# Row sums of the gated rows taken earlier, one conversion moved to ScalarE, and an opening in half tiles

## The chip, the cores and the metric

One core of one Trainium2 chip. The metric is the time of one execution in device microseconds; smaller is better. Each timed execution also reports its span and its mean granted TensorE clock: 1.000 is full clock, 0.5 is half.

## The reference, cut to what matters

A block of a transformer over 2048 rows of 1024: layer norm, local attention, output product with a residual, layer norm, then a bilinear feed-forward with 3584 hidden columns.

```python
x = A_x
h = x + _A_ref(_layernorm(x, axis=-1), A_wqkv, A_wo)
h2 = h + _B_ref(_layernorm(h, axis=-1), B_w_gate, B_w_up, B_w_down)
# _B_ref: g = x @ w_gate; u = x @ w_up; return (g * u) @ w_down
```

The change touches the start (the first layer norm and the first product with `wqkv`) and the last down product.

## The kernel before: the parts concerned

The opening takes the first 512 rows as four row tiles. Each is normalized on VectorE, transposed on TensorE in two halves, copied out of PSUM (one half by ScalarE, one by VectorE) and multiplied with the first weight tile. That weight tile comes in two transfers of 512 KB: products 1 to 16 of a row tile need the first, 17 to 32 the second.

```python
load_x0(0)
load_x0(1)
load_w0(0, 4)          # first half of the weight tile
load_x0(2)
load_w0(4, 4)          # second half
load_x0(3)
# ... (13 products on a zero tile follow, to warm the array) ...
for t in range(4):
    if t < 3:
        first_half(t + 1, 0)
    first_norm(t)
    if t < 3:
        first_half(t + 1, 1)
    if t > 0:
        first_mm(t - 1, range(0, 6))
    first_transpose(t)
    first_copy(t)
    if t > 0:
        first_mm(t - 1, range(6, 8))
    if t < 3:
        first_rstd(t + 1)
```

The last down product works on two chunks of rows at once with seven products of half-size blocks in place of eight, in 16-bit floats. Weights and gated rows are scaled by powers of two that come from sums of absolute values. Row sums need one reduction on VectorE (`rows`), one product with ones on TensorE (`total`) and five small VectorE operations. The b and t tiles are quarters of the down weights and their differences; each is held as two tiles, such as t2a and t2b. dx and dy are the accumulators of this product in PSUM; h is the residual to which its results are added.

```python
conv_down(down["b12"])                                   # VectorE, 2 instructions
# ...
add_homes(t1v, Fv("b12"), Fv("b11"), ALU.subtract)       # VectorE, 2 of 1.94 us
scale_h.rows()                                           # VectorE, 2 small ones
conv_down(down["b21"])                                   # VectorE, 2
for q in range(4):
    dprod(ps_x[q], q, HA["11"], fcells(down["b11"]), True)   # TensorE, 14 products
    if q == 1:
        scale_h.total(ps_y[3])
        # ...
for q in range(4):
    nc.scalar.activation(ps_y[q][:], ps_x[q][:], ACTF.Copy, scale=sh)
# ... HF22, HF21 on VectorE, HF11 on ScalarE, S1 = HF21 + HF22 on VectorE ...
for q in range(4):
    dprod(ps_x[q], q, HA["12"], fcells(down["b21"]), False)
    result(2, q, 0, ps_x[q], scale_d.inv, None)          # VectorE, waits for dprod q
    if q == 2:
        conv_down(down["b22"])                           # VectorE, 2
# ... HF21 = HF11 - HF21, HF11 = S1 - HF11 on VectorE ...
add_homes(t2v, Fv("b22"), t1v, ALU.subtract)             # t2a, t2b
for q in range(4):
    dprod(ps_x[q], q, S1, cells(t1h), True)
# ...
for q in range(4):
    dprod(ps_y[q], q, HF["11"], cells(t2h), False)       # waits for t2a, then t2b
```

Of the kernel before, what the change touches and what calls it, by code (L numbers as in the profile page):

```python
# [8 lines left out]
BF = mybir.dt.bfloat16  # L9
# [3 lines left out]
ALU = mybir.AluOpType  # L13
# [5 lines left out]
D = 1024  # L19
# [59 lines left out]
def kernel(  # L79
# [11 lines left out]
    nc = tc.nc  # L91
# [9 lines left out]
    lnp = ctx.enter_context(tc.tile_pool(name="ln", bufs=4))  # L101
# [80 lines left out]
    def normalize(src, mv4, rs4, t):  # L182
        ln = lnp.tile([128, D], BF, tag="ln")
        nc.vector.tensor_scalar(ln[:], src[:], mv4[:, t, 0:1], rs4[:, t:t + 1], ALU.subtract, ALU.mult)
        return ln

    def ln_tiles(name):
        mv4 = small.tile([128, 4, nc.vector.BN_AGGR_DIM], F32, tag="mv4", name="mv" + name)
        rs4 = small.tile([128, 4], F32, tag="rs4", name="rs" + name)
        return mv4, rs4  # L190
# [9 lines left out]
    lnTs = {}  # L200
# [59 lines left out]
    x0 = [hp.tile([128, D], BF, tag="h", name=f"x0_{t}") for t in range(4)]  # L260
# [29 lines left out]
        nc.gpsimd.memset(mask[:, w, 0:DIL * w], NEG)  # L290

    wps = psum.tile([128, 512], F32, tag="mm", name="warm_ps")
    for i in range(13):
        nc.tensor.matmul(wps[:], lhsT=warm[:, 0:128], rhs=warm[:], start=True, stop=True)

    qkv_in = {}
# [19 lines left out]
    lnTs[0] = lnTp.tile([128, KO, TC], BF, tag="lnT", name="lnT1_0")  # L316
    mv0, rs0 = ln_tiles("1_0")

    pts = {}

    sts = {}

    def first_half(t, i):
        if i == 0:
            sts[t] = small.tile([128, 2, nc.vector.BN_STATS_DIM], F32, tag="st", name=f"st0_{t}")
        nc.vector.bn_stats(out=sts[t][:, i, :], in_=x0[t][:, bass.ts(i, 512)])

    def first_rstd(t):
        nc.vector.bn_aggr(out=mv0[:, t, :], in_=sts[t][:])
        rstd_of(mv0, rs0, t, t + 1)  # L330

    lns = {}

    def first_norm(t):
        lns[t] = normalize(x0[t], mv0, rs0, t)

    def first_transpose(t):
        for hf in range(2):
            pt = psum.tile([128, KO // 2, 128], BF, tag="mm", name=f"pt{t}_{hf}")
            for kk in range(KO // 2):  # L340
                nc.tensor.transpose(pt[:, kk, :], lns[t][:, bass.ts(4 * hf + kk, 128)], ident[:])
            pts[t, hf] = pt
        nc.scalar.copy(lnTs[0][:, 0:4, bass.ts(t, 128)], pts[t, 0][:])

    def first_copy(t):
        nc.vector.tensor_copy(lnTs[0][:, 4:8, bass.ts(t, 128)], pts[t, 1][:])

    def first_mm(t, kos):
        for ko in kos:
            for j in range(4):  # L350
                nc.tensor.matmul(ps0[j][:, bass.ts(t, 128)], lhsT=wts["qkv", 0][:, ko, bass.ts(j, 128)],
                                 rhs=lnTs[0][:, ko, bass.ts(t, 128)], start=(ko == 0), stop=(ko == KO - 1))
# [5 lines left out]
# [6 lines that stand above are left out]
        if t > 0:  # L364
            first_mm(t - 1, range(0, 6))
        first_transpose(t)
        first_copy(t)
        if t > 0:
            first_mm(t - 1, range(6, 8))
        if t < 3:  # L370
            first_rstd(t + 1)
# [187 lines left out]
    scale_gu, scale_d, scale_h = Scale("gu", 56), Scale("d", 56), Scale("h", 56)  # L559
# [216 lines left out]
    NH = NF // 4  # L776
# [8 lines left out]
    def to_f16(dst, src, sc, eng=nc.vector):  # L785
        if eng is nc.scalar:
            nc.scalar.activation(dst, src, ACTF.Copy, scale=sc)
        else:
            eng.tensor_scalar(dst, src, sc, None, ALU.mult)

    def f16(ap):
        return ap.bitcast(F16)

    def conv_down(homes):
        for t in homes:
            to_f16(f16(t[:, 0:NH, :]), t[:, 0:NH, :], scale_d.s)

    def cells(homes):
        return [t[:, k, :] for t in homes for k in range(NH)]
# [1 line left out]
    down = {}  # L801
    for n in range(NP):
        if n + 1 < NP:
            weight_sums(n + 1)
            if n + 2 < NP:
                load_pair(n + 2)
            else:
                names = ("b11a", "b12a", "b21a", "b21b", "b12b")
                ws = {k: home(wpool, "w", "dn_" + k, BF) for k in names}
                down["b11"] = [ws["b11a"], home(att, "oD", "dn_b11b", BF)]  # L810
                down["b12"] = [ws["b12a"], ws["b12b"]]
                down["b21"] = [ws["b21a"], ws["b21b"]]
                load_down(down["b11"], 0, 0)
                load_down(down["b12"], 0, 1)
        else:
            load_down(down["b21"], 1, 0)
        sums = [] if n == 0 else [
            (lambda n=n, k=k: abs_sum_h(n - 1, k, h23[4 * (n - 1) + k])) for k in range(4)]
        pair_block(n, h23[4 * n:4 * n + 4], sums)
        if n == NP - 2:  # L820
            conv_down(down["b11"])
# [9 lines left out]
    def add_homes(dst, x0, x1, op):  # L831
        for d, a0, a1 in zip(dst, x0, x1):
            nc.vector.tensor_tensor(d, a0, a1, op)
# [4 lines left out]
    def dprod(ps, q, lhs, rhs, fresh, lo=0, n=TC):  # L838
        for k in range(NP):
            nc.tensor.matmul(ps[:, bass.ds(lo, n)], lhsT=lhs[k][:, bass.ts(q, 128)], rhs=rhs[k][:, bass.ds(lo, n)],  # L840
                             start=(fresh and k == 0), stop=(k == NP - 1), skip_group_check=not fresh)

    def fcells(homes):
        return [f16(c) if c.dtype != F16 else c for c in cells(homes)]

    def result(c, q, hf, ps, sc, other, lo=0, n=TC):
        rows = (hs2 if c == 2 else hs3)[q]
        cols = bass.ds(hf * 512 + lo, n)
        nc.vector.scalar_tensor_tensor(rows[:, cols], ps[:, bass.ds(lo, n)], sc,
                                       rows[:, cols] if other is None else other[:, bass.ds(lo, n)], ALU.mult, ALU.add)  # L850
        nc.sync.dma_start(outf[bass.ds(c * TC + q * 128, 128), cols], rows[:, cols])


    conv_down(down["b12"])
    t1v = [t[:, 0:NH, :] for t in t1h]
    t2v = [t[:, 0:NH, :] for t in t2h]
    add_homes(t1v, Fv("b12"), Fv("b11"), ALU.subtract)
    scale_h.rows()
    conv_down(down["b21"])
    for q in range(4):  # L860
        dprod(ps_x[q], q, HA["11"], fcells(down["b11"]), True)
# [9 lines left out]
    for k in range(NP):  # L871
        to_f16(HF["22"][k], HA["22"][k], sh)
        to_f16(HF["21"][k], HA["21"][k], sh)
    s1h = [t[:, 0:NH, :] for t in down["b11"]]
    S1 = fcells(down["b11"])
    for k in range(NP):
        to_f16(HF["11"][k], HA["11"][k], sh, nc.scalar)
    for k in range(NP):
        nc.vector.tensor_tensor(S1[k], HF["21"][k], HF["22"][k], ALU.add)
    for q in range(4):  # L880
        dprod(ps_x[q], q, HA["12"], fcells(down["b21"]), False)
        result(2, q, 0, ps_x[q], scale_d.inv, None)
        if q == 2:
            conv_down(down["b22"])
    for k in range(NP):
        nc.vector.tensor_tensor(HF["21"][k], HF["11"][k], HF["21"][k], ALU.subtract)
    for k in range(NP):
# [60 lines left out]
```

## Time and profile before

| | before |
|---|---|
| time, median of 3 | 787.76 us |
| span of the profiled execution | 785.4 us |
| TensorE busy | 773.4 us, 98% |
| TensorE's waits that the profile names | 5.7 us in all |
| first full-width product (end of the opening) | 16.95 us |
| tail: first dx product to last dy product | 692.61 to 781.74, 89.13 us |

The prediction shows the lines and how they were read.

### The profile page before, as it was taken

What the parts mean: (1) busy time and instruction counts of PE and PEld (TensorE: products, weight loads), DVE (VectorE), ACT (ScalarE), POOL (GpSimd) and SP (SyncE); (2) the same over time, 40 slices, a digit from 0 to 9 for tenths busy, and PEclk for the clock granted to TensorE, in tenths of its full rate; (3) what the DMA queues carried; (4) which work ended last, traced back from release to release, by engine and by line L of the source; (5) the groups of instructions that cost most, each with busy time, mean ns of one, the idle gap of its engine ahead of it and who ended that gap; (6) DMA issues with size and microseconds to landing.
All of it is one profiled execution on the core that took longest, in us unless ns stands there. A gap on an engine that the chain in (4) does not pass through costs nothing.

```text
span 785.4 us, 10283 instructions
## 1 busy us (share of the span) xinstructions
PE 773.4 (98%) x3672; PEld 358.1 (46%) x3734; DVE 586.5 (75%) x729; ACT 394.8 (50%) x913; POOL 150.8 (19%) x160
## 2 busy tenths in 40 slices
PE   9999999999999999999999999999999999989998
PEld 6544444444444444444444444444444444434444
DVE  6629999999899998999979962724444453589862
ACT  4627445313676653956666510116777677645240
POOL 0000000100000200002000010067768668500000
PEclk9999999999999999999999999999999999999999
DMA  7999693996956868869455599533332332820001
GB/s 265 263 227 215 164 283 85 277 279 160 338 175 199 273 237 224 259 197 306 148 161 194 164 207 305 126 105 86 86 108 56 107 98 63 281 95 28 1 28 53
DMA packets 183683, 135.94 MB, mean 173 GB/s; under 512 B 79056, under 2 KB 176464, under 8 KB 181584
## 3 DMA queue, kind: packets, MB, share of 16 engines
q1 hardware_dynamic: 180048, 113.27, 51.0%
q0 software_dynamic: 3584, 22.02, 8.2%
q8 instruction: 29, 0.48, 0.3%
q14 instruction: 22, 0.18, 0.1%
HBM read 106.95 MB, written 22.02 MB: 164 GB/s over the span
## 4 chain that ended last, share of the span: by engine, by line
PE 75%; DVE 21%; issue 1%; SPq 1%; DMA 1%; ACT 0%; DVEq 0%
PE pu L389 12%; PE acc L608 12%; PE pg L389 12%; PE pz L661 6%; PE py L661 6%; PE px L661 6%; PE wo L510 5%; DVE prod L429 4%; PE ps L389 3%; PE dx L840 3%; PE pv L661 3%; PE dy L840 3%; DVE pv L472 2%; DVE prod L431 2%; SPq L223 1%
## 5 line engine op out<-in xcount | busy, mean ns | idle before, releaser
L389 PE MATMUL ps<-lnT,w_qkv 128*128 128x512 bf16 x721 | 158.9, 379 | 0.8
L389 PEld LDWEIGHTS <-w_qkv 128*128 128x128 bf16 x736 | 71.9, 98 | 85.9 <-issue 0.2
L389 PE MATMUL pu<-lnT,w_wu 128*128 128x512 bf16 x438 | 105.1, 379 | 0.6
L389 PE MATMUL pg<-lnT,w_wg 128*128 128x512 bf16 x440 | 105.1, 379 | 0.4
L608 PE MATMUL acc<-w_wd,gs 128*128 128x512 bf16 x438 | 96.7, 379 | 0.5
L300 ACT CAST sg<-ps 128x512 bf16<-128x512 f32 x96 | 54.8, 590 | 53.2 <-PE ps L389 49.4
L472 DVE TENSOR_TENSOR pv<-vD,at 128x4096 bf16<-128x4096 bf16 x32 | 72.5, 2287 | 0.3
L429 DVE TENSOR_TENSOR prod<-qD,kD 128x4096 bf16<-128x4096 bf16 x32 | 72.4, 2284 | 0.1
L608 PEld LDWEIGHTS <-gs 128*128 128x128 bf16 x448 | 43.8, 98 | 52.9
L661 PEld LDWEIGHTS <-sw 128*128 128x128 f16 x448 | 43.8, 98 | 52.8
L389 PEld LDWEIGHTS <-w_wg 128*128 128x128 bf16 x448 | 43.8, 98 | 52.9
L389 PEld LDWEIGHTS <-w_wu 128*128 128x128 bf16 x448 | 43.8, 98 | 52.9
L179 ACT ACTIVATE rs<-mv,eps 128x1 f32<-128x1 f32 x32 | 9.5, 296 | 102.0 <-DVE mv L176 98.2
L588 ACT CAST us<-pu 128x512 bf16<-128x512 f32 x56 | 33.1, 591 | 50.5 <-PE pu L389 49.3
L510 PE MATMUL wo<-w_wo,oT 128*128 128x512 bf16 x251 | 55.6, 379 | 0.3
L661 PE MATMUL px<-lnT,ws 128*128 128x512 bf16 x211 | 52.6, 379 | 0.6
L661 PEld LDWEIGHTS <-ws 128*128 128x128 f16 x336 | 32.9, 98 | 39.6
L484 POOL DMA_DIRECT2D od<-oD x4 | 2.2, 542 | 249.8 <-DVE oD L482 162.5
L640 POOL TENSOR_TENSOR sw<-ws 128x512 f16<-128x512 f16 x28 | 32.3, 1153 | 87.9 <-PE acc L608 47.2
L583 ACT CAST gs<-pg 128x512 bf16<-128x512 f32 x56 | 33.1, 591 | 12.8 <-PE pg L389 8.7
L510 PEld LDWEIGHTS <-oT 128*128 128x128 bf16 x256 | 25.0, 98 | 30.2
L431 DVE TENSOR_TENSOR prod<-prod 128x4096 bf16<-128x4096 bf16 x16 | 36.6, 2288 | 0.3
(244 smaller groups left out, 1189.4 us busy)
## 6 DMA issues: line engine op xcount, KB each, us to landing
w_wg<-in_B_w_gate_dram SPq DMA_DIRECT2D x14, 1024.0 KB, 6.9
w_wu<-in_B_w_up_dram SPq DMA_DIRECT2D x14, 1024.0 KB, 5.3
w_wd<-in_B_w_down_dram SPq DMA_DIRECT2D x16, 896.0 KB, 7.8
w_wo<-in_A_wo_dram SPq DMA_DIRECT2D x8, 1024.0 KB, 7.5
w_pair<-in_B_w_gate_dram SPq DMA_DIRECT2D x14, 512.0 KB, 4.0
w_pair<-in_B_w_up_dram SPq DMA_DIRECT2D x14, 512.0 KB, 5.3
w_qkv<-in_A_wqkv_dram SPq DMA_DIRECT2D x5, 1024.0 KB, 9.5
kd<-sg SPq DMA_DIRECT2D x32, 144.0 KB, 2.8
```

The costliest lines, as they stand in the source:

```text
L300: nc.scalar.copy(sg[:, HB:HB + TC], ps[:])
L389: nc.tensor.matmul(ps[:], lhsT=wt[:, ko, bass.ts(j, 128)], rhs=rhs[:, ko, :], start=(ko == 0), stop=(ko == KO - 1))
L429: nc.vector.tensor_tensor(prod[:, j], qD[:], kD[:, :, o:o + SUB], ALU.mult)
L431: nc.vector.tensor_tensor(prod[:, :, 0:16], prod[:, :, 0:16], prod[:, :, 16:32], ALU.add)
L472: nc.vector.tensor_tensor(pv[:, j], vD[:, :, o:o + SUB], at[:, w, None, :].to_broadcast((128, DH, SUB)), ALU.mult)
L510: nc.tensor.matmul(ps[:], lhsT=oTs[c][:, kk, t, :], rhs=wts["wo", c, hf][:, kk, :], start=(kk == 0), stop=(kk == KO - 1))
L583: nc.scalar.copy(gs[:], pg[:])
L588: nc.scalar.copy(us[:], pu[:])
L608: nc.tensor.matmul(acc[t][:], lhsT=hT[f][:, bass.ts(t, 128)], rhs=wts["wd", c, hf, b][:, j, :], start=(f == 0), stop=(f == NF - 1))
L640: nc.gpsimd.tensor_tensor(sw[:, i, 0], a21, a22, ALU.add)
L661: nc.tensor.matmul(ps[:], lhsT=lhs[:, ko, :], rhs=rhs[:, ko, :], start=(fresh and ko == 0), stop=(ko == 3), skip_group_check=not fresh)
L840: nc.tensor.matmul(ps[:, bass.ds(lo, n)], lhsT=lhs[k][:, bass.ts(q, 128)], rhs=rhs[k][:, bass.ds(lo, n)], start=(fresh and k == 0), stop=( ...
```

## The change

Its intent in the tail: take the row sums early enough that TensorE need not stop for them, and take the b22 conversion off VectorE. In the opening: shorter steps from a row tile to its first product, with two warm-up products fewer.

```diff
-    for i in range(13):
+    for i in range(11):
         nc.tensor.matmul(wps[:], lhsT=warm[:, 0:128], rhs=warm[:], start=True, stop=True)
@@ first_norm
-        lns[t] = normalize(x0[t], mv0, rs0, t)
+        lns[t] = lnp.tile([128, D], BF, tag="ln", name=f"ln0_{t}")
+        for i in range(2):
+            cols = bass.ts(i, 512)
+            nc.vector.tensor_scalar(lns[t][:, cols], x0[t][:, cols], mv0[:, t, 0:1], rs0[:, t:t + 1],
+                                    ALU.subtract, ALU.mult)
@@ first_transpose (first_copy, VectorE's copy of the second half, is gone)
-            pts[t, hf] = pt
-        nc.scalar.copy(lnTs[0][:, 0:4, bass.ts(t, 128)], pts[t, 0][:])
+            nc.scalar.copy(lnTs[0][:, bass.ts(hf, 4), bass.ts(t, 128)], pt[:])
@@ the tail
+    scale_h.rows()
     add_homes(t1v, Fv("b12"), Fv("b11"), ALU.subtract)
-    scale_h.rows()
@@
         to_f16(HF["11"][k], HA["11"][k], sh, nc.scalar)
+    conv_down(down["b22"], nc.scalar)
@@
-        if q == 2:
-            conv_down(down["b22"])
```

## The prediction

> **What bounds the kernel now.** I read the page first: shares, then the chain that ended last.
>
> ```profile
> PE 773.4 (98%) x3672; PEld 358.1 (46%) x3734; DVE 586.5 (75%) x729; ACT 394.8 (50%) x913; POOL 150.8 (19%) x160
> PE 75%; DVE 21%; issue 1%; SPq 1%; DMA 1%; ACT 0%; DVEq 0%
> ```
>
> TensorE is busy in 98% of the span, so this change can only recover its few idle microseconds. I therefore asked for the list of waits, TensorE's alone:
>
> ```profile
> PE dy L547 <- DVE rowbh L543: 2.5, 1, 2.5
> PE warm_ps L294 <- DVE warm L280: 1.2, 1, 1.2
> PE dy L840 <- DVE h L849: 0.6, 1, 0.6
> PE dy L840 <- DVE dn_t2a L833: 0.6, 1, 0.6
> PE ps L351 <- ACT lnT L343: 0.5, 1, 0.5
> PE dy L840 <- DVE dn_t2b L833: 0.3, 1, 0.3
> ```
>
> Columns: total, times, longest. The change aims at the first (the sum over ones that gives the scale of the gated rows, L547) and the fifth (the first product of the opening). Lines four and six lie behind the first, in the same tail. What sets the tail's end is in the chain of waits, in order of time (start, us, what):
>
> ```profile
> 698.96 1.94 DVE dn_t1b L833
> 700.89 0.13 DVE rowh L542
> ...
> 718.26 1.06 DVE dn_b22a L789
> 719.32 0.54 DVE dn_b22b L789
> ...
> 732.37 1.95 DVE dn_t2b L833
> 734.32 0.04 issue
> 734.36 10.73 PE dy L840 x49
> ```
>
> From 692.81 to 734.32 the chain stays on VectorE; TensorE takes over only at 734.36. So the 2.5 us wait at L547 is not on it: TensorE idles there, runs on, and idles again for t2a and t2b. A gain must shorten VectorE's queue.
>
> For the opening I read the timeline, then the second half of the first weight tile (w_qkv, issued 2.69), then a table of stretches limited to the products (columns: us, TensorE busy, weight loads busy, clock, DMA share, GB/s):
>
> ```profile
> 7.22 0.58 ACT L343 COPY lnT<-pt 128x512 bf16<-128x512 bf16 x1 [1.58 <-PE pt L341]
> 7.86 1.62 PE L351 MATMUL ps<-lnT,w_qkv 128*128 128x128 bf16 x24 [0.45 <-ACT lnT L343]
> ```
>
> ```profile
> DMA to landing us min/median/max: 6.1/6.1/6.1
> ```
>
> ```profile
> 8.30:8.70 0.40, 0.40 (x11) 0.40 (x8) 1.00 0.12 44
> 8.70:8.85 0.15, 0.15 (x4) 0.04 (x2) 1.00 0.07 27
> 8.85:9.30 0.45, 0.45 (x10) 0.45 (x8) 1.00 0.02 9
> ```
>
> The second half lands at 2.69 + 6.1 = 8.8. Weight loads run solid before and after, but only 0.04 of 0.15 us in 8.70 to 8.85: product 17, the first that needs that half, waits about 0.1 us for the transfer although the opening is still late. An earlier start meets that landing.
>
> **What the Trainium skill says.** "TensorE: Matmul & The Clock Gate", Part 1 (What's actually happening): the array starts at half clock and is released after about 3.4 us of activity in a free-running window. The trace agrees: the weight loads of the 13 warm-up products start 0.43 us apart, while 512-column products later start 0.216 apart (7 in 1.51). So the warm-up buys clock, and 11 may risk it. "ScalarE: Activation LUTs", Rules for kernel authors: VectorE is up to about 3 times faster per bf16 element on such scalings. The trace agrees: one 128x512 scaling starts every 0.61 us on ScalarE (14 from 708.32 to 716.99) and every 0.26 on VectorE. "DMA: Bandwidth & Descriptors", Queues, rings and completion order: a copy is split over up to 16 engines, each counting separately, so the slowest engine sets the landing. This is why I take the landing and not the bandwidth; no view here shows the engines apart.
>
> **The change, part by part: the tail.**
> (a) scale_h.rows() moves ahead of the two t1 subtractions. Its sources are ready: the last absolute sum on ScalarE ends at 696.36 + 0.19 = 696.55 and VectorE gets there at 696.94. It is 0.32 us of work (700.81 to 701.13), moved and not removed. The row sums are then ready near 697.3; TensorE reaches the total after its second group, whose last product starts at 698.43 and holds the array 0.216: 698.65 in place of 701.26. TensorE is 2.6 us earlier. VectorE is not: conversion of b12, rows, t1, b21 and the five small operations are the same sum in another order, and the scale is ready at 704.05 as before.
> (b) The conversion of b22 leaves VectorE: start of its first instruction to start of the one after its second, 720.31 - 718.18 = 2.13 us. What follows moves up only if its inputs do. result(q=3) needs TensorE's q=3 group, which ends near 719.8 and with (a) at 717.2: ready. The L886 subtractions need ScalarE's HF11: ScalarE waits 1.84 us for TensorE before its fourth scaling (L869), a wait that (a) removes, so HF11 ends near 715.2 rather than 717.0: ready. So t2a, now done at 732.37, is done at 730.24, and t2b at 732.19 instead of 734.32.
> (c) ScalarE gains two 128x3584 conversions. From 0.61 us for 512 columns and 1.07 for 1024 (both absolute sums), each further 512 costs 0.46: 0.61 + 6 x 0.46 = 3.4 us, 6.7 for both, an estimate. It runs 715.2 to 722, in a gap (its next work was dp at 722.84). t2a needs b22a at 728.2, with over 6 us to spare. dp is not urgent.
> (d) TensorE: its S1 products end at 731.71 - 2.6 = 729.1, it waits for t2a until 730.29 (1.2 us), runs seven products (1.51) to 731.80 and waits for t2b until 732.23 (0.4). It started that second half at 734.36: gain 2.13 us. After that only TensorE is on the chain until the last store, and the 2.13 goes through. (a) alone would give nothing, as TensorE would wait longer for t2a; (b) alone almost nothing, as result(q=3) and all VectorE work behind it would wait for TensorE until 719.8.
>
> **The opening.** Two warm-up products less: 0.85 us of cold array, ending near 5.9 in place of 6.72. Half a row tile normalized: the 512-column scaling of L789 has a duration of 0.35 against 0.55 for the 1024 here, so the first transposes start near 6.2, 0.5 earlier. They now run on the cold array (0.107 each instead of mostly 0.056), so the four end near 6.8, ScalarE's copy near 7.4, and the first product starts near 7.5 against 7.86: 0.36 earlier. Sixteen products at 0.056 bring product 17 to 8.4, where it waits for the landing at 8.8 and starts at 8.85, as before. After that the rhythm is 40 array operations of 0.056 per row tile plus the wait for the first copy, 2.40 us (transposes at 9.31, 11.71, 14.11). The second copy on ScalarE ends some 0.5 us behind the first and is needed 0.9 behind; the next row scale comes 0.25 later on ScalarE, which the half tile gives back. I book 0.1 us for the opening, up to 0.4 where the transfer lands earlier in executions without a profile.
>
> Sum: 787.76 - 2.13 - 0.1 = 785.5.
>
> **The rivals.**
> 1. All waits count: 2.45 at L547, 0.9 for t2a and t2b, 0.45 in the opening: 3.8 us, so 784.0. For it: these are TensorE waits on a TensorE-bound kernel. Against: the chain shows VectorE holding the tail to 734.3, and of its work only 2.13 goes.
> 2. A new wait eats the tail: ScalarE, nearly solid from 704 to 722, delays HF11 or b22, or VectorE's sequencer, which handles ten separate semaphore waits ahead of L886 (about 0.1 us each in the chain, 719.86 to 720.81), is exposed when nothing covers them. Against: the inputs lead by a wide margin, over 3 us for HF11 and 6 for b22; the semaphore waits start once q=3 has arrived and lie under the last two result instructions. It would leave 786.5 to 787.7.
> 3. The opening loses: with 11 warm-ups and a short pause, the clock is released a window later. Sixteen products at 0.107 instead of 0.056 cost 0.8 us, partly in the shadow of the landing: up to +0.5, 786.0.
>
> **Range and chances.** The tail's 2.1 is firm to about 0.4; the opening lies between -0.4 and +0.5; the three timed runs spread 0.9 us. That gives 784.6 to 786.8. Two per cent would be 15.8 us, and TensorE has only 12 idle in all (785.4 - 773.4), so faster by over 2% is 0.5%, slower 0.5%, within 99%.
>
> **What the changed profile would show.** Right: no wait at L547; VectorE's t2a starting about 2.1 us earlier relative to the first dx product; waits for t2a of about 1.2 and t2b of 0.4, so larger than now; b22 on ScalarE at 3.4 us each; the first product near 7.5, yet product 17 at the landing and the first full-width product (L389) near 17 as before. Wrong: a tail shorter by more than 2.3 us (VectorE was not the limit); idle time of VectorE ahead of L886 or t2a (rival 2); 128-column products 0.107 apart after 7.5 (rival 3); an opening 0.4 us shorter (the landing did not bind).

## The result, and the profile after

| | before | changed |
|---|---|---|
| time, median of 4 | 787.65 us | 785.16 us (784.94 to 787.53) |
| ratio | | 0.9976, interval 0.9954 to 0.9997 |
| tail: first dx product to last dy product | 89.13 us | 86.98 us |
| first full-width product, profiled execution | 16.95 us | 19.38 us |

The profiled execution of the changed kernel was its slowest, 787.53 us at a mean clock of 0.997; the other three took 784.94 to 785.27 us at 1.000. Its tail can be read; its opening is an exception: in the six other profiles with this opening (runs 4 to 9), the first full-width product starts between 16.33 and 17.61.

TensorE's waits in the changed kernel (total, times, longest):

```profile
PE ps L349 <- DMA w_qkv<-in_A_wqkv_dram: 2.1, 2, 1.0
PE warm_ps L294 <- DVE warm L280: 1.2, 1, 1.2
PE dy L837 <- DVE dn_t2a L830: 1.0, 1, 1.0
PE dy L837 <- DVE h L846: 0.6, 1, 0.6
PE dy L837 <- DVE dn_t2b L830: 0.3, 1, 0.3
```

The wait for the row sums is gone. The wait for t2a has grown from 0.6 to 1.0: part of what TensorE no longer waits for there, it waits for here. The first line is new: in this profile the opening waits for its weights, once before product 1 and once before product 17. That is no mark of the new opening alone: product 17 waits for the same transfer in runs 3, 11 and 12, which have the old one (0.62, 1.03 and 0.94 us). The chain of waits, in order of time, and ScalarE's two new instructions in the timeline (start, us, what):

```profile
732.75 1.95 DVE dn_t2b L830
734.70 0.04 issue
734.74 10.73 PE dy L837 x49
```

```profile
717.46 3.28 ACT L784 ACTIVATE dn_b22a<-dn_b22a,sbd 128x3584 f16<-128x3584 bf16 x1
720.63 3.29 ACT L784 ACTIVATE dn_b22b<-dn_b22b,sbd 128x3584 f16<-128x3584 bf16 x1
```

VectorE still hands the tail to TensorE, at t2b. Counted from the tail's first dx product (695.14 here, 692.61 before) that happens at 734.74 - 695.14 = 39.60 in place of 734.36 - 692.61 = 41.75: 2.15 us earlier, and the tail is 2.15 shorter to its end. So the tail gave 2.15 of the 2.49 us between the medians, and in this execution the opening took it back: the tail began 2.53 us later than before. The next lines show how: the chain in the opening, then stretches of 1 us (busy time and count of TensorE, weight loads, VectorE, ScalarE and GpSimd; clock; DMA share; GB/s).

```profile
2.69 7.12 DMA w_qkv<-in_A_wqkv_dram
```

```profile
8.80:9.80 1.00, 0.01 (x1) 0.00 (x0) 1.00 (x4) 0.00 (x0) 0.00 (x0) 0.97 0.21 80
9.80:10.80 1.00, 0.95 (x10) 0.95 (x11) 0.96 (x3) 0.00 (x0) 0.19 (x1) 0.50 0.01 4
...
12.80:13.80 1.00, 1.00 (x18) 1.00 (x16) 0.92 (x3) 0.05 (x1) 0.00 (x0) 0.82 1.07 379
```

The second half of the weight tile landed at 2.69 + 7.1 = 9.8, a full microsecond later than in the profile of before; TensorE stood still for 1.04 us, after 1.03 us ahead of product 1, and then the array ran at half clock. From the clock column (the two stretches left out show 0.50 too): 0.97 is 0.06 us at half, 0.50 the whole stretch, 0.82 is 0.36 us, so from 9.74 to 13.16, 3.4 us.

### The profile page after: what moved, and what is told of

It reads as the page before. It is cut to its first block, busy times and chain, and to the rows that moved or that the text cites. A ratio compares the mean times of both kernels' runs of the same rounds, so it can differ in the third digit from the quotient of the medians.

```text
span 785.8 us, 10287 instructions
## 1 busy us (share of the span) xinstructions
PE 774.1 (99%) x3670; PEld 359.2 (46%) x3732; DVE 583.6 (74%) x727; ACT 402.9 (51%) x919; POOL 150.9 (19%) x160
## 3 DMA queue, kind: packets, MB, share of 16 engines
q0 software_dynamic: 3584, 22.02, 8.1%
## 4 chain that ended last, share of the span: by engine, by line
PE 74%; DVE 20%; issue 2%; SPq 1%; DMA 1%; ACT 0%; DVEq 0%
PE pu L386 12%; PE acc L605 12%; PE pg L386 12%; PE pz L658 6%; PE py L658 6%; PE px L658 6%; PE wo L507 5%; DVE prod L426 4%; PE ps L386 3%; PE pv L658 3%; PE dx L837 3%; PE dy L837 3%; DVE pv L469 2%; DVE prod L428 2%; SPq L223 1%
```

## The experiments

The theory: the tail's gain of 2.1 us is all there is, it needs both parts of the tail change, and the opening gives nothing because the weight transfer binds it. Every run was timed in 5 rounds; times are medians of 5 executions (6 in run 12; 9 or 11 of the kernel before beside them). Runs 1 to 4, 5 to 8 and 9 to 11 shared a chip each, where the kernel before took 787.76, 788.29 and 788.39 us. All results are correct but for two that are wrong.

**Run 1: the row sums alone.** The change's edit to `scale_h.rows()` on the kernel before, nothing else.

```diff
+    scale_h.rows()
     add_homes(t1v, Fv("b12"), Fv("b11"), ALU.subtract)
-    scale_h.rows()
```

> Only the row sums are moved ahead of the t1 subtractions. My theory (VectorE's queue sets the tail): the 2.5 us wait of TensorE at the total (L547) vanishes and comes back whole as a longer wait for t2a (0.6 before, about 3.1 now, with 0.4 for t2b unchanged); time the same as before within 0.2 us. Rival (TensorE's waits count): about 2.5 us faster.

Measured: 788.28 us, ratio 1.0005 (0.9993 to 1.0018). TensorE's wait, and stretches around it (columns as above):

```profile
PE dy L840 <- DVE dn_t2a L833: 3.1, 1, 3.1
```

```profile
729.00:732.00 3.00, 0.16 (x1) 0.00 (x0) 3.00 (x5) 0.69 (x1) 0.00 (x0) 1.00 0.00 0
732.00:735.00 3.00, 2.70 (x9) 1.12 (x9) 3.00 (x3) 0.00 (x0) 0.00 (x0) 0.70 0.00 0
```

The wait moved whole, as expected: VectorE is solid in both stretches. What I had not expected stands in the clock column. After a pause of 3.1 us the array ran at half clock for a while (0.70 on average in 732 to 735, 0.74 in 735 to 738, 1.00 after that), and the tail of this execution grew to 90.37 us, 1.24 more than before. Three of the five executions show a mean clock of 0.998 (788.28 to 788.95), the two at 1.000 took 787.52 and 787.73, the time of before.

**Run 2: b22 on ScalarE alone.**

```diff
+    conv_down(down["b22"], nc.scalar)       # behind the HF11 loop
-        if q == 2:
-            conv_down(down["b22"])
```

> Only the conversion of b22 goes to ScalarE; the row sums stay behind t1. My theory (the two parts need each other): VectorE's last result of the first group (q=3) waits for TensorE until about 27 us after the tail's first dx product, so the subtractions behind it start no earlier; gain at most 0.2 us, a new idle time of VectorE of about 1.5 us ahead of that result. Rival (VectorE's load alone counts): up to 1.1 us faster, as TensorE loses its waits for t2a and t2b.

Measured: 787.19 us, ratio 0.9992 (0.998 to 1.0005); tail 88.66 us, 0.47 shorter. VectorE's last result of the group in the timeline:

```profile
719.88 0.75 DVE L849 SCALAR_TENSOR_TENSOR h<-dx,ibd,h 128x512 bf16<-128x512 f32 x1 [1.55 <-PE dx L840]
```

The idle time of 1.55 us is as expected: VectorE is free earlier and waits for TensorE. The gain is not 0.2 but 0.47. That result starts at 719.88 in place of 720.31, and the subtractions follow it at once (720.54, before 720.97): the semaphore waits ahead of them overlapped with the result instruction. The 0.47 is of one trace; the interval of the ratio includes 1.

**Run 3: both parts of the tail, the old opening.**

> Both parts of the tail, the old opening. My theory: 2.1 us faster than before, the whole gain of the change (ratio near 0.9973). Rival (the tail gives half, the opening the rest): 1.0 to 1.6 us faster.

Measured: 785.36 us, ratio 0.9968 (0.9955 to 0.998); tail 86.98 us, 2.15 shorter, the same as in the changed kernel. Apart the parts give nothing and 0.47, together 2.15: each removes what would have eaten most of the other's gain.

**Run 4: the opening alone.**

> Only the opening changed. My theory (the landing of the second half of the first weight tile bounds it): within 0.4 us of before, product 17 starts just after that landing, the wait before it longer than the 0.1 us of before. Rival (the opening gains by itself): 0.4 to 0.6 us faster. Rival (fewer warm-ups leave the array cold, as in the profile of the changed kernel): some executions slower by 0.5 us or more with a mean clock below 1.000.

Measured: 787.55 us, ratio 1.0 (0.9987 to 1.0014). One of five executions had a clock of 0.998. TensorE in the timeline:

```profile
7.24 1.05 PE L349 MATMUL ps<-lnT,w_qkv 128*128 128x128 bf16 x16 [0.27 <-ACT lnT L344]
8.79 0.62 PE L349 MATMUL ps<-lnT,w_qkv 128*128 128x128 bf16 x8 [0.50 <-DMA w_qkv<-in_A_wqkv_dram]
...
16.97 4.26 PE L386 MATMUL ps<-lnT,w_qkv 128*128 128x512 bf16 x19
```

The first product starts at 7.24 in place of 7.86, and product 17 waits 0.50 us for a transfer that lands at 2.69 + 6.1 = 8.8. The full-width products start at 16.97, before at 16.95. Measured from product 17, the opening needs 8.18 us here and in runs 5 and 7, but 8.10 with the old opening (before and runs 1, 3, 11): 0.08 more, as the row tiles follow each other in 2.44 us and no longer 2.40.

The profiles also show what the prediction took for fixed: with the old opening the first product starts anywhere from 7.33 to 7.87 (seven profiles). It follows the end of the 13 warm-up products, which took 5.23 to 5.73 us: they start 0.43 us apart until the clock is released, and the release comes at a different time in each execution. (The clock column reads 1.00 there all the same; it does not show this cold start.) With the changed opening TensorE mostly waits for the normalized rows instead, and the first product starts from 7.22 to 7.33 in six profiles of seven. So in the profiles both openings are at product 17 before its weights, by 0.1 to 1.0 us.

**Run 5: the changed kernel again.**

> The changed kernel once more. My theory (the tail gives all, the opening nothing): 785.2, the same as with the tail alone (785.36) within 0.3; in the profile product 17 starts just after the second half of the first weight tile lands. Rival (the opening with fewer warm-ups loses clock, as in the changed kernel's first profile): executions above 787 with a mean clock of 0.997 or 0.998 again, in two or more of five.

Measured: 784.85 us, ratio 0.996 (0.9947 to 0.9972), executions from 784.46 to 786.12, none with the clock loss of the first profile. Tail 87.00 us. Product 17 starts at 9.13, just behind its landing:

```profile
9.13 0.62 PE L349 MATMUL ps<-lnT,w_qkv 128*128 128x128 bf16 x8 [0.85 <-DMA w_qkv<-in_A_wqkv_dram]
...
17.31 1.89 PE L386 MATMUL ps<-lnT,w_qkv 128*128 128x512 bf16 x7
```

Against run 3 on another chip that is 0.5 us less, outside the 0.3 expected, and against before the ratio says 3.2 us, more than the tail's 2.15. Five of the nine executions of before beside it show a clock of 0.998; run 12 follows that up.

**Run 6: the second half of the weight tile loaded earlier.**

```diff
     load_w0(0, 4)
-    load_x0(2)
     load_w0(4, 4)
+    load_x0(2)
     load_x0(3)
@@ in the loop, for t == 1
-            first_half(t + 1, 0)
         first_norm(t)
+            first_half(t + 1, 0)
```

> The changed kernel with the second half of the first weight tile loaded ahead of row tile 2 (and that tile's statistics taken after the normalization of tile 1). My theory (the landing binds the changed opening): the half lands about 0.7 us earlier, product 17 starts at 8.1 to 8.4 in place of 8.8, the time falls by 0.3 to 0.5 us to 784.8. Rival (the landing only seems to bind, row statistics or ScalarE's two copies do): no gain, or a loss of some tenths.

Measured: 785.47 us, ratio 0.9964 (0.9952 to 0.9977): no gain over run 5. From the timeline:

```profile
8.80 0.62 PE L349 MATMUL ps<-lnT,w_qkv 128*128 128x128 bf16 x8 [0.53 <-DMA w_qkv<-in_A_wqkv_dram]
9.43 1.29 DVE L324 BATCH_NORM_STATS2 st<-x 128x6 f32<-128x512 bf16 x2 [0.57 <-DMA x<-in_A_x_dram]
12.03 0.72 PE L343 MATMUL pt<-ident,ln 128*128 128x128 bf16 x8 [0.21 <-DVE ln L336]
```

My number failed: the half was issued 0.55 us earlier but took 6.6 us, so it landed at 2.14 + 6.6 = 8.7. That is 0.35 before the landing in run 5's profile and hardly before the 8.8 of run 4's. The row tile that had stepped back now came late, TensorE's transposes of it waited 0.21 us, and the full-width products started at 17.32, where run 5 had 17.31. These transfers share one queue (q1 moved 6.76 of the 6.77 MB of the first 24 us in the profile of before), and this exchange of places only moved the wait.

**Runs 9 and 10: no need for the second half (wrong result).** The same edit on the changed kernel (run 9) and on run 3's, with the old opening (run 10):

```diff
-                nc.tensor.matmul(ps0[j][:, bass.ts(t, 128)], lhsT=wts["qkv", 0][:, ko, bass.ts(j, 128)],
+                nc.tensor.matmul(ps0[j][:, bass.ts(t, 128)], lhsT=wts["qkv", 0][:, ko % 4, bass.ts(j, 128)],
```

> Wrong result on purpose: the changed kernel with products 17 to 32 of each row tile of the opening reading the first half of the weight tile again, so that they need not wait for the second half. My theory (the landing binds the opening): the wait ahead of product 17 vanishes, it starts near 8.15, and the opening ends 0.4 to 0.9 us earlier than in the changed kernel, depending on when its transfer lands. Rival (something else binds, such as the statistics of row tile 2 that wait for their own transfer): tile 1's transposes wait instead and the gain is under 0.2 us.

> Wrong result on purpose: the same edit on the old opening (with the changed tail). My theory: here product 17 starts between 8.35 and 8.75, the full-width products start 0.3 us or so later than in the changed opening with the same edit. That difference is what the changed opening is worth when the landing does not bind; the prediction worked out 0.36. Rival (the changed opening is worth nothing even then): no difference, or the old one ahead, as its row tiles follow each other in 2.40 us against 2.44.

Measured: 785.0 us (run 9) and 784.21 us (run 10), ratios 0.9963 and 0.9951. TensorE in run 9, then in run 10:

```profile
7.23 1.50 PE L349 MATMUL ps<-lnT,w_qkv 128*128 128x128 bf16 x24 [0.35 <-ACT lnT L344]
...
16.33 2.97 PE L386 MATMUL ps<-lnT,w_qkv 128*128 128x512 bf16 x13
```

```profile
7.61 1.50 PE L351 MATMUL ps<-lnT,w_qkv 128*128 128x128 bf16 x24 [0.45 <-ACT lnT L343]
...
16.59 2.75 PE L389 MATMUL ps<-lnT,w_qkv 128*128 128x512 bf16 x12
```

With the transfer out of the way the products run through (24 in one piece), and the opening ends at 16.33, against 17.31 in run 5. The landing does bind, in the traces; the median of run 9 is not below run 5's 784.85 (another chip). And here the changed opening is worth something: 0.38 us at the first product (7.61 against 7.23), of which three row tiles at 0.04 more take 0.12 back, so 0.26. That is one pair of profiles, and the old opening alone scatters by 0.54 us at that place; the means of all profiles but the changed kernel's first, 7.58 and 7.25, would leave 0.2. The times do not show that order: run 9 is the slower one by 0.8 us. Only one execution of each is traced, and those two are 0.1 apart in span (782.7 and 782.8), so what the other executions of run 9 lost stays open. Which of the opening's three edits (fewer warm-up products, half tiles, both copies on ScalarE) does what was not tested.

**Runs 7, 8 and 11: a version that beats both.** If VectorE still sets the tail, more work off VectorE should pay. ScalarE idles ahead of the scale, so b21 goes there too, and the result that waits longest for TensorE moves behind the subtractions, which do not need it. Run 7 is this on the changed kernel, run 8 adds run 6's edit, run 11 has it with the old opening.

```diff
-    conv_down(down["b21"])
+    conv_down(down["b21"], nc.scalar)
@@
         dprod(ps_x[q], q, HA["12"], fcells(down["b21"]), False)
-        result(2, q, 0, ps_x[q], scale_d.inv, None)
+        if q < 3:
+            result(2, q, 0, ps_x[q], scale_d.inv, None)
@@
         nc.vector.tensor_tensor(HF["21"][k], HF["11"][k], HF["21"][k], ALU.subtract)
+    result(2, 3, 0, ps_x[3], scale_d.inv, None)
```

> The changed kernel with b21 converted by ScalarE too, in its idle time before the scale is known, and the last of the first results moved behind the first subtractions. My theory (VectorE's queue still sets the tail after the change, TensorE's waits for t2a and t2b of 1.0 and 0.3 us show by how much): both waits vanish, 1.4 to 1.6 us faster than the changed kernel, 783.7. Rival (TensorE or ScalarE has become the limit): at most 0.5 us.

> Both of the last two together. If they are independent, as an opening and a tail under the same bound should be, their gains add: 1.8 to 2.0 us faster than the changed kernel, 783.3.

> The faster tail (b21 on ScalarE as well) with the old opening. If the changed opening is worth nothing as it stands: 783.6, the same as with the changed opening within 0.3. Rival (it is worth some tenths, hidden by noise so far): 784.0 or more.

Measured: 783.59 us (run 7, ratio 0.9942), 784.09 (run 8, 0.9944), 783.97 (run 11, 0.9944). TensorE's waits in run 7, all of them:

```profile
PE pt L343 <- DVE ln L336: 1.2, 1, 1.2
PE warm_ps L294 <- DVE warm L280: 1.2, 1, 1.2
PE ps L349 <- DMA w_qkv<-in_A_wqkv_dram: 1.1, 1, 1.1
PE dy L837 <- DVE h L846: 0.6, 1, 0.6
PE ps L349 <- ACT lnT L344: 0.4, 1, 0.4
```

Both t2 waits are gone, and the tail is 85.38 us, 1.62 shorter than run 5's. The median fell by 1.26. In run 7's profile the weight half landed later than in run 5's (product 17 at 9.43 against 9.13); whether the rest of the difference lies there in the other executions is not shown. The two edits of this run were not tried apart. Run 8 missed its 783.3: as run 6 gained nothing there was nothing to add. Run 11 came out 0.38 above run 7, on another chip: a little outside the 0.3 expected, and just short of the rival's 784.0, so the times do not decide. The two profiles do for their own executions: the second weight half took 6.7 us to land in both, and the full-width products start at 17.56 (run 11) and 17.61 (run 7).

**Run 12: the kernel before again.**

> The kernel before, unchanged, to catch one of its executions with a mean clock of 0.998 (12 of its 27 timed ones so far) in a trace. My theory: TensorE's pause of 2.45 us at the total (L547) fills most of one of the clock's windows, and the array runs at half clock for one window of about 3.4 us behind it; if the profiled execution shows 0.998, the products behind L547 are 0.43 us apart instead of 0.216. Rival: the clock is lost elsewhere (the opening, as in the changed kernel's first profile). If the profiled execution shows 1.000, this stays open. Time 787.7 without the loss, about 788.6 with it.

Measured: 787.58 us, ratio 0.9996 (0.9983 to 1.0009). The profiled execution is one with 0.998, 788.82 us. Stretches of 4 us around the total (columns as above):

```profile
698.00:702.00 4.00, 1.55 (x8) 0.58 (x7) 3.96 (x5) 0.00 (x0) 0.00 (x0) 1.00 0.29 92
702.00:706.00 4.00, 4.00 (x13) 1.45 (x12) 3.86 (x14) 1.24 (x2) 0.00 (x0) 0.57 0.00 0
706.00:710.00 4.00, 4.00 (x20) 1.84 (x19) 4.00 (x16) 0.81 (x2) 0.00 (x0) 1.00 0.00 0
```

TensorE idles 2.45 us for the row sums in the first stretch; in the second it runs 13 products where the third runs 20, at a clock of 0.57. If that is half clock and full clock, as in the changed kernel's opening (0.50 and 1.00), 0.57 over 4 us is 3.4 us at half; run 1's two stretches make 3.4 us too. All other stretches of this execution show 1.00. Its tail took 90.34 us, 1.21 more than the 89.13 at full clock. (The windows of the expectation are those of the page that the prediction names, "TensorE: Matmul & The Clock Gate", Part 1; no trace here shows a window, only the 3.4 us at half clock.)

So the wait that the chain had left out does cost time in some executions. Over the runs 21 of 44 executions of the kernel before show 0.998 (the count of 12 in 27 in the expectation should have been 13); their median is 788.61 us, that of the other 23 is 787.53. Runs 2 and 4 keep the pause, and 1 of their 10 executions shows it. In the kernels with the row sums moved, run 1 aside, 2 of 44 executions fell below 0.999, one of them in the opening, as shown. On the second chip, side by side, it was 5 of 9 before against none of 20. Where the clock was lost in the executions without a profile is not traced, so that it was at the total there too is likely and not shown.

## Why the prediction was right

Predicted were 785.5 us and a gain of 2.2; measured were 785.16 and, in the traces, 2.15 from the tail. That the sum is as close as 0.3 us is in part luck: the 0.1 booked for the opening did not come, and the clock that the change spares, some 0.5 us on average (an estimate: 21 of 44 times 1.1), was not in it.

- **Tail, steps (a), (b) and (d).** TensorE reaches the total without a wait, VectorE's queue is shorter by the b22 conversion, and t2b is ready 2.15 us earlier where 2.13 were worked out. TensorE's waits for t2a and t2b came out at 1.0 and 0.3 us, worked out as 1.2 and 0.4. That (a) alone gives nothing held (run 1). That (b) alone gives almost nothing was a little low: 0.47 (run 2).
- **ScalarE, step (c).** 3.28 and 3.29 us for the halves of b22, estimated at 3.4, in the gap foreseen. The Trainium skill would have been closer than my extrapolation from two absolute sums: "ScalarE: Activation LUTs", Rules for kernel authors, budgets about 0.3 us plus 0.83 ns per element, an estimate of 3.27 us for 3584 columns.
- **Opening.** The mechanism was right: an earlier first product meets the landing. The sizes were not. The first product starts at 7.22 to 7.33, not near 7.5: in five of those six profiles the clock was released before the transposes (8 in 0.72 us), which I had put on the cold array, and in the sixth (run 4) they were cold but began at 5.96, not 6.2; with the old opening it starts from 7.33 to 7.87, not always at 7.86. In the traces with a binding landing the changed opening costs 0.08 us where I booked a gain of 0.1. Without the landing it was worth 0.26 in one pair of profiles (the 0.36 lacked the slower rhythm). Of what I quoted on the clock, the trace bears out the two rates, not the 3.4 us: in the profile of before all 13 warm-up products ran cold.
- **Rivals.** That all of TensorE's waits count failed in run 1: the largest went and no time with it. That ScalarE or VectorE's semaphore waits eat the tail failed in run 3. That the opening loses clock came true in the first profile of the changed kernel, but not as foreseen: products 1 to 16 ran at full clock, and the loss came behind two pauses for late transfers. Whether two warm-up products more would have prevented it is not tested.
- **What was missed.** I called the 2.5 us wait worthless because it is not on the chain. In an execution at full clock that is so. In the traced one of run 12 it cost the array its clock and 1.21 us of tail; about half of all executions of before (21 of 44) lost clock, and 1.1 us by the medians (788.61 against 787.53). The removal of that risk is, by these counts, a second gain of the change, which the single trace of before, at clock 1.000, could not show. It accounts for part of run 5's larger gain: five in nine of 1.1 us are 0.6 of the 1.0 us beyond the tail's 2.15.

## What to carry to other kernels

Two waits in a row in front of one engine can be one problem: here the first was taken away and the second grew by as much (2.5 and 0.6 became 3.1 us), until the engine that both stem from had less to do. Work out the ready time of every input of the next step, and see which of two parts of a change gives nothing without the other. And look at the granted clock of every execution, not only of the profiled one: a pause off the critical path (2.45 us in run 12) can still make what comes behind it slower.

## What the Trainium skill lacked or had wrong

- "TensorE: Matmul & The Clock Gate", HAM oscillation: it gives the rule "no PE-idle gaps >~3.4µs". Here a pause of 2.45 us was enough to lose the clock (run 12), and two pauses of 1.03 and 1.04 us with 16 products between them in the opening of the changed kernel. That the windows run free, as Part 1 of the page says, fits with its striking in only some executions; no trace shows them.
- "DMA: Bandwidth & Descriptors": no section says how far the landing of one and the same transfer scatters. The second weight half, issued at 2.68 or 2.69 in twelve profiles, landed after 5.8 to 7.1 us.
